# Attention, a dense FFN and a top-1 MoE in one kernel: routed weights in blocks of 128 rows, expert layers by halves, first expert's columns by tile, and products without readers in the last tile's waits

## The chip, the cores and the metric

The kernel runs on one core of one Trainium2 chip. The metric is the device time of one execution in microseconds, as the median of three runs. Engines are named as in the profile: PE (TensorE) does matrix products, PEld is the loading of their stationary operand, DVE, ACT and POOL are the vector, scalar and GpSimd engines, and SP issues most DMAs.

## The reference

Three layers follow each other on 1536 tokens of 512 numbers, all in fp32 accuracy.

```python
# 1 attention: B=2, H=8, S=768, D=64; a token sees 4 sinks and the last 128 positions
scores = where(is_sink | in_window, q @ k.T / sqrt(D), -1e9)
x = softmax(scores) @ v                       # -> [1536, 512]
# 2 dense FFN, w_in 512x2048, w_out 2048x512
h = x @ w_in
x = maximum(0.01 * h, h) @ w_out
# 3 routed, 8 experts, w1 512x1024, w2 1024x512
do_compute = x @ w_skip > 0
logits = x @ w_gate;  e = argmax(logits);  gate = softmax(logits)[e]
out = x + (do_compute ? gate * (maximum(x @ w1[e], 0) @ w2[e]) : 0)
```

## The kernel before

**Products.** Each operand is split into a rounded part (hi) and the rest (lo), and a product is three PE products: hi·hi, hi·lo and lo·hi. ACT (or POOL) writes the hi part and DVE (or POOL) the lo part (`split` for weights, lines 701 and 708; `split_psum`, lines 1094 and 1095).

**Order.** A planner (`Plan`) takes every operation with its engine, a modelled cost, the buffers it reads and writes and a due time `pr`, and makes one fixed order for each engine. The queues are in order: an instruction that waits holds back all behind it. Buffers are taken by tag and have few slots: 32 slots of split weights (`w`), 4 of raw weights (`wm`), 1 `vs`, 2 `wf`, and PSUM banks `acc` 2, `h` 2, `T` 2, `S` 1, `PV` 1.

**Dense layers.** Attention and the dense FFN go in six groups of 256 tokens (two tiles of 128 tokens), the FFN in chunks of its 2048 columns (`chunk`: lines 835 and 856). After a group its gating follows (`gating`): copy x out of PSUM (902 on ACT, 904 on DVE), transpose it (918), split it (921, 922), make nine logits a token (w_skip and eight gates) with twelve products a tile on a nine-column stationary operand (930), copy them (935), transpose them back (937), then on DVE the argmax chain (947 to 959) to a one-hot row (954), and on PE a count of earlier tokens with the same expert (977), from which DVE reads each token's place in its expert's list (983, `rank_all`). Finished rows are scattered to a list in HBM, 128 places an expert. The last group does this for its two tiles one after the other.

**First expert.** Expert 0's 128 rows would have to come back from that list. Instead the ten earlier tiles' rows come by an early load (`xs0`), and `first_x` adds the rows of the last two tiles on PE: four 128-column pieces of transposed x are the sum of a product with `xs0` (817) and of a product of each last tile with a 0/1 matrix `sel` (819), which DVE makes from the rank (987).

**Routed layers.** `plan_routed` runs the eight experts on 128 rows each: weights come in tiles of 512 KB (four for w1, four for w2; loads at 1037), are split (701, 708), x is loaded (1050; not for expert 0's products) and transposed (1059), the first layer is 24 products of 512 columns in two banks, hidden columns 0 to 511 and 512 to 1023 (1066), relu is done by ACT on the one and DVE on the other (1070, 1071), then eight transposes (1075), their split, 24 products of the second layer (1082), gate and residual (1085), and a scatter to the output.

Of the kernel before, what the change touches and what calls it, by code (L numbers as in the profile page):

```python
# [47 lines left out]
C_TR = 114.0  # L48
# [177 lines left out]
class Arm:  # L226
# [63 lines left out]
    def keep(self):  # L290

        k = lambda name, shape, dt=F32: self.pool.tile(shape, dt, tag=name, bufs=1, name=name)
        self.oh_all = k("oh_all", [128, self.NT // 128, self.E], BF16)
        self.rank_all = k("rank_all", [128, self.NT // 128])
        self.gate_all = k("gate_all", [128, self.NT // 128])
        self.nt = k("nt", [128, 2, self.E])
        self.tot = k("tot", [128, 2], I32)
        self.w9 = k("w9", [128, 2, 4, 9], F32R)
        self.ks = k("ks", [128, self.KD, 16])
# [393 lines left out]
    def split(self, src, dst, at, n, pr, hi="ACT", lo="DVE", view=lambda t: t):  # L693
# [12 lines left out]

        P.op(hi, {"ACT": c_act(n, False), "DVE": c_dve2(n), "POOL": c_pool1(n)}[hi], f_hi, r=[src], w=[hk], pr=pr)
        P.op(lo, {"DVE": c_dve(n), "POOL": c_pool2(n)}[lo], lambda: eng[lo].tensor_tensor(  # L708
            out=at(1), in0=view(src.tile), in1=at(0).bitcast(F32), op=ALU.subtract), r=[src, hk], w=[lk], pr=pr)
# [36 lines left out]
    def plan_dense(self):  # L746
# [50 lines left out]
        for step in self.rest:  # L797
            step()
# [11 lines left out]
    def first_x(self, x2):  # L810
# [4 lines left out]
        self.x0 = [P.buf(t, [128, 128]) for t in ("h", "h", "acc", "acc")]  # L815
        for k, x in enumerate(self.x0):
            P.op("PE", 220, lambda k=k, x=x: nc.tensor.matmul(out=x.tile, lhsT=xs0.tile[:, k:512:4], rhs=c["idt"], start=True, stop=False), r=[xs0], w=[x], pr=pr - 0.1)
        for k, x in enumerate(self.x0):
            P.op("PE", 440, lambda k=k, x=x: [nc.tensor.matmul(out=x.tile, lhsT=x2[i].tile[:, k:512:4], rhs=sel.tile[:, i, :], start=False, stop=i == 1) for i in range(2)],
                 r=[(x2[i], h) for i in range(2) for h in range(2)] + [(sel, 0), (sel, 1)], w=[x], pr=pr)  # L820
# [43 lines left out]
    def prepare(self, done):  # L864
# [9 lines left out]
        P.op("DVE", 90, lambda: nc.vector.tensor_copy(self.w9[:, 0], raw.tile), r=[raw], w=["w9"], pr=8)  # L874
        P.op("DVE", 100, lambda: nc.vector.tensor_tensor(out=self.w9[:, 1], in0=raw.tile, in1=self.w9[:, 0].bitcast(F32), op=ALU.subtract), r=[raw], w=["w9"], pr=8)
# [10 lines left out]
    def gating(self, g, acc, own):  # L886
# [9 lines left out]
        for i, t in zip(own, tiles):  # L896
            x = P.buf("x2", [128, 514])
            x2.append(x)
            for h in range(parts):
                q = slice(w * h, w * h + w)  # L900
                if (i if n > 1 else h) == 0:
                    P.op("ACT", c_act(w, True), lambda x=x, i=i, q=q: nc.scalar.activation(out=x.tile[:, q], in_=acc[i].tile[:, q], func=AF.Copy), r=[acc[i]], w=[(x, h)], pr=pr - 8)
                else:
                    P.op("DVE", c_dve(w), lambda x=x, i=i, q=q: V.tensor_copy(x.tile[:, q], acc[i].tile[:, q]), r=[acc[i]], w=[(x, h)], pr=pr - 8)
# [3 lines left out]
        lp = P.buf("T", [9, 128 * n])  # L908
        for m, x in enumerate(x2):
            tp = P.buf("T", [128, 512])  # L910
            xh = P.buf("wl", [128, 2, 512], F32R)
            for h in range(parts):
# [7 lines left out]
                P.op("PE", len(ks) * C_TR, tr, r=[(x, h)], w=[(tp, h)], pr=pr, hold=[xh])  # L920
# [3 lines left out]
            for h in range(parts):  # L924
                ks = range(4 // parts * h, 4 // parts * (h + 1))

                def lg(m=m, xh=xh, ks=ks):
                    for k in ks:
                        for j, (a, b) in enumerate(((0, 0), (1, 0), (0, 1))):
                            nc.tensor.matmul(out=lp.tile[:, 128 * m:128 * m + 128], lhsT=self.w9[:, a, k, :], rhs=xh.tile[:, b, 128 * k:128 * k + 128],  # L930
                                             start=k == 0 and j == 0, stop=k == 3 and j == 2)

                P.op("PE", 3 * len(ks) * 54, lg, r=[(xh, (0, h)), (xh, (1, h)), "w9"], w=[lp], pr=pr)
        ls = P.buf("wl", [9, 128 * n])
        P.op("ACT", c_act(128 * n, True), lambda: nc.scalar.activation(out=ls.tile, in_=lp.tile, func=AF.Copy), r=[lp], w=[ls], pr=pr)
        lt = P.buf("T", [128, n, 9])
        P.op("PE", 30 * n, lambda: [nc.tensor.transpose(lt.tile[:, m, :], ls.tile[:, 128 * m:128 * m + 128], c["idt"][0:9, 0:9]) for m in range(n)], r=[ls], w=[lt], pr=pr)
# [10 lines left out]
        d(70, lambda: V.tensor_scalar(out=v(act, 1), in0=lt.tile[:, :, 0:1], scalar1=0.0, scalar2=None, op0=ALU.is_gt), [lt], [(s, "act")])  # L948
        for m in range(n):
            d(80, lambda m=m: V.scalar_tensor_tensor(out=cand()[:, m, :], in0=lt.tile[:, m, 1:9], scalar=one(mx, m), in1=c["em"][:, 0, :], op0=ALU.is_equal, op1=ALU.mult),  # L950
              [lt, (s, "mx")], [(s, ("cand", m))])
        d(85, lambda: V.tensor_reduce(out=v(mi, 1), in_=cand(), op=ALU.min, axis=AX.X), [(s, ("cand", m)) for m in range(n)], [(s, "mi")])
# [18 lines left out]
        for m, x in enumerate(x2):  # L971
# [8 lines left out]
            for part in ([ts[:-1], ts[-1:]] if last else [ts]):  # L980
                P.op("PE", 30 * len(part), lambda part=part, count=count: count(part), r=[("oh", t) for t in part], w=[cp], pr=pr)
            rk = self.rank_all[:, tiles[m]:tiles[m] + 1]
            d(80, lambda m=m, rk=rk, cp=cp: V.tensor_tensor_reduce(out=cand()[:, m, :], in0=cp.tile, in1=oh(m), op0=ALU.mult, op1=ALU.add,
                                                                   scale=1.0, scalar=0.0, accum_out=rk), [cp, ("oh", tiles[m])], [(s, ("cand", m)), ("rank", tiles[m])])
            if last:
                i = own[0]
                d(133, lambda rk=rk, i=i: V.tensor_scalar(out=self.sel.tile[:, i, :], in0=self.sel.tile[:, 2, :], scalar1=rk,
                                                          scalar2=self.sel.tile[:, 3, i:i + 1], op0=ALU.is_equal, op1=ALU.mult),
                  [("rank", tiles[m]), (self.sel, 2), (self.sel, ("own", i))], [(self.sel, i)])
# [29 lines left out]
    def plan_routed(self):  # L1019
# [4 lines left out]
        def weights(e, m, pr):  # L1024
            src = io["moe2_w2"][e].rearrange("(p j) d -> p j d", j=8) if m else io["moe2_w1"][e].rearrange("(p k) f -> p k f", k=4)
            W[e, m] = []
            for n in range(4):
                sv = src[:, 2 * n:2 * n + 2, :].rearrange("p j d -> p (j d)") if m else src[:, n, :]
# [5 lines left out]
                for i in range(k):  # L1034
                    q = slice(1024 // k * i, 1024 // k * (i + 1))
                    raw = P.buf(tag, [128, 1024 // k])
                    P.op("SP", C_DMA, lambda raw=raw, sv=sv, q=q: nc.sync.dma_start(out=raw.tile, in_=sv[:, q]), w=[raw], pr=pr - 16, lat=512 * 1024 / 310.0 / k)
                    self.split(raw, [(x, i) for x in hl], lambda j, hl=hl, q=q: hl[j].tile[:, q], 1024 // k, pr + 0.3 * n, "ACT", "DVE" if n != 3 or e == self.E - 1 else "POOL")
# [4 lines left out]
        for e in range(self.E):  # L1043
            pr = N + 3.5 * e
            if e + 1 < self.E:
                weights(e + 1, 0, pr - 2.8)
            weights(e, 1, pr - 1.5)
# [6 lines left out]
            if e == 0:  # L1054
                for k, x in enumerate(self.x0):
                    self.split_psum(x, (xt, k), lambda i, xt=xt, k=k: xt.tile[:, i, k], 128, N - 9)
            else:
                tp = P.buf("acc", [128, 4, 128])
                P.op("PE", 4 * C_TR, lambda xs=xs, tp=tp: [nc.tensor.transpose(tp.tile[:, k, :], xs.tile[:, k:512:4], c["idt"]) for k in range(4)], r=[xs, ("g1", e - 1)], w=[tp], pr=pr - 3.48)
                self.split_psum(tp, xt, lambda i, xt=xt: xt.tile[:, i], 512, pr - 6)  # L1060
            hp = [P.buf(t, [128, 512]) for t in (("S", "PV"), ("h", "h"))[e % 2]]
            for k in range(4):
                def g1(k=k, xt=xt, hp=hp, w1=w1):
                    for a in range(2):
                        for n, (i, j) in enumerate(((0, 0), (0, 1), (1, 0))):
                            nc.tensor.matmul(out=hp[a].tile, lhsT=xt.tile[:, i, k, :], rhs=w1[k][j].tile[:, 512 * a:512 * a + 512],  # L1066
                                             start=k == 0 and n == 0, stop=k == 3 and n == 2)
                P.op("PE", 6 * c_mm(512), g1, r=([(xt, (k, 0)), (xt, (k, 1))] if e == 0 else [xt]) + [w1[k][0], w1[k][1]], w=hp + ([("g1", e)] if k == 2 else []), pr=pr + 0.01 * k)
# [4 lines left out]
            for b in range(2):  # L1073
                tp = P.buf("T", [128, 4, 128])
                P.op("PE", 4 * C_TR, lambda hs=hs, tp=tp, b=b: [nc.tensor.transpose(tp.tile[:, j, :], hs.tile[:, 4 * b + j:1024:8], c["idt"]) for j in range(4)], r=[hs], w=[tp], pr=pr + 0.065)
                self.split_psum(tp, (gt, b), lambda i, gt=gt, b=b: gt.tile[:, i, 4 * b:4 * b + 4, :], 512, pr - 3)
            yp = P.buf("acc", [128, 512])
            for n in range(4):
# [5 lines left out]
                P.op("PE", 6 * c_mm(512), g2, r=[(gt, (n // 2, 0)), (gt, (n // 2, 1)), w2[n][0], w2[n][1]], w=[yp], pr=pr + 3.55 + 0.01 * n)  # L1084
# [6 lines left out]
    def split_psum(self, src, dst, at, n, pr):  # L1091
        P, nc = self.p, self.nc
        hk, lk = self.halves(dst)
        P.op("ACT", c_act(n, True), lambda: nc.scalar.activation(out=at(0), in_=src.tile, func=AF.Copy), r=[src], w=[hk], pr=pr)
        P.op("DVE", c_dve(n), lambda: nc.vector.tensor_tensor(out=at(1), in0=src.tile, in1=at(0).bitcast(F32), op=ALU.subtract), r=[src, hk], w=[lk], pr=pr)
# [219 lines left out]
def constants(nc, cp, pool, c, n_sink, window, E):  # L1315
# [21 lines left out]

    G.iota(dif, pattern=[[-1, 128]], base=0, channel_multiplier=1, allow_small_or_imprecise_dtypes=True)
# [80 lines left out]
```

## Time and profile before

| | before |
|---|---|
| timed runs, us | 560.93, 560.33, 559.50; median 560.33 |
| profiled execution, us | 561.0 (its span in the trace 559.2) |
| PE busy | 521.8 us, 93% of the span |
| DVE, ACT, POOL busy | 74%, 62%, 30% |
| moved by DMA | 72.5 MB |
| up to 433 us | attention and the dense FFN, group by group |
| 433 to 457 us | from the last dense product to expert 0's second layer |
| 457 to 551 us | experts, then 8 us to the end of the span |

A time in the trace is counted from the span's start. A group of instructions on one line (x12) has one start and one busy time. In the chain of waits each piece is what the end of the program waited for at that time. In the timeline a number in brackets is idle time of the engine just before, with what ended it. The granted clock (PEclk, or the column of that name) is 1.00 at TensorE's upper level of 2.4 GHz and 0.50 at its lower of 1.2 GHz.

### The profile page before, as it was taken

What the parts mean: (1) busy time and instruction counts of PE and PEld (TensorE: products, weight loads), DVE (VectorE), ACT (ScalarE), POOL (GpSimd) and SP (SyncE); (2) the same over time, 40 slices, a digit from 0 to 9 for tenths busy, and PEclk for the clock granted to TensorE, in tenths of its full rate; (3) what the DMA queues carried; (4) which work ended last, traced back from release to release, by engine and by line L of the source; (5) the groups of instructions that cost most, each with busy time, mean ns of one, the idle gap of its engine ahead of it and who ended that gap; (6) DMA issues with size and microseconds to landing.
All of it is one profiled execution on the core that took longest, in us unless ns stands there. A gap on an engine that the chain in (4) does not pass through costs nothing.

```text
span 559.2 us, 10360 instructions
## 1 busy us (share of the span) xinstructions
PE 521.8 (93%) x3370; PEld 457.7 (82%) x3370; DVE 415.9 (74%) x1167; ACT 345.8 (62%) x899; POOL 166.9 (30%) x288
## 2 busy tenths in 40 slices
PE   3899999999998999989999999999999789999994
PEld 2778998888887888978888888988898668878883
DVE  3899999997667676777576876766856558998761
ACT  3998766655666656675556766465555367767650
POOL 4332022130264133333223333220221314354231
PEclk9999999999999999999999999999999899999998
DMA  7996344431111212232112320106565359879820
GB/s 179 308 349 234 130 154 139 136 104 38 50 39 30 68 30 45 50 83 49 29 24 51 85 49 16 24 1 221 164 213 184 128 193 319 301 236 353 277 79 19
DMA packets 80351, 72.46 MB, mean 130 GB/s; under 512 B 56563, under 2 KB 64755, under 8 KB 80288
## 3 DMA queue, kind: packets, MB, share of 16 engines
q1 hardware_dynamic: 78000, 70.54, 40.7%
q0 software_dynamic: 1600, 1.04, 0.6%
q8 instruction: 29, 0.48, 0.3%
q14 instruction: 34, 0.28, 0.2%
q10 hardware_dynamic: 688, 0.13, 0.1%
HBM read 65.40 MB, written 10.51 MB: 136 GB/s over the span
## 4 chain that ended last, share of the span: by engine, by line
PE 66%; DVE 14%; ACT 9%; issue 4%; DMA 3%; POOL 2%; POOLq 0%; SPq 0%; DVEq 0%; ACTq 0%
PE h L835 17%; PE acc L856 14%; PE acc L1082 7%; PE T L616 3%; PE PV L655 3%; PE h L1066 2%; DMA wm<-in_moe_w_dram 2%; PE S L1066 2%; PE PV L1066 2%; ACT P L588 2%; PE S L582 2%; DVE w L708 2%; PE T L930 1%; DVE C L671 1%; DVE P L585 1%
## 5 line engine op out<-in xcount | busy, mean ns | idle before, releaser
L835 PE MATMUL h<-x,w 128*128 128x256 f32 x1128 | 155.1, 286 | 0.1
L835 PEld LDWEIGHTS h<-x,w 128*128 128x128 f32 x1128 | 143.9, 190 | 4.3 <-DVE w L708 0.6
L856 PE MATMUL acc<-w,gh 128*128 128x512 f32 x308 | 100.2, 406 | 0.2 <-ACT gh L848 0.2
L588 ACT ACTIVATE P<-P,s 128x272 f32<-128x272 f32 (+1 forms) x96 | 50.2, 524 | 27.8 <-DVE s L585 26.4
L600 POOL TENSOR_SCALAR P<-P,s 128x272 f32<-128x272 f32 (+1 forms) x72 | 36.8, 523 | 93.8 <-DVE s L593 74.9
L856 PE MATMUL acc<-w,gl 128*128 128x512 f32 x156 | 61.5, 394 | 0.6 <-DVE gl L849 0.6
L856 PEld LDWEIGHTS acc<-w,gh 128*128 128x128 f32 x308 | 53.2, 189 | 7.9 <-ACT gh L848 0.6
L708 DVE TENSOR_TENSOR w<-wm,w 128x1024 fp32r<-128x1024 f32 x35 | 52.3, 1509 | 8.8 <-ACT w L701 8.0
L701 ACT ACTIVATE w<-wm 128x1024 fp32r<-128x1024 f32 x44 | 46.1, 1060 | 17.2 <-DMA wm<-in_moe_w_dram 6.8
L847 DVE TENSOR_TENSOR h<-h,t 128x256 f32<-128x256 f32 x94 | 40.2, 427 | 22.2 <-ACT t L846 21.7
L846 ACT ACTIVATE t<-h 128x256 f32<-128x256 f32 x94 | 35.7, 379 | 33.5 <-PE h L835 33.2
L848 ACT ACTIVATE gh<-h 128x256 fp32r<-128x256 f32 x92 | 34.9, 379 | 21.7 <-DVE h L847 20.9
L849 DVE TENSOR_TENSOR gl<-h,gh 128x256 fp32r<-128x256 f32 x92 | 38.6, 419 | 9.3 <-ACT gh L848 8.5
L701 ACT ACTIVATE w<-wf 128x512 fp32r<-128x512 f32 x52 | 31.8, 627 | 11.1 <-DVE wf L741 8.9
L585 DVE CUSTOM_DVE_ANT_0 P<-S,mk 128x272 f32<-128x272 f32 (+1 forms) x70 | 28.9, 413 | 11.3 <-PE S L582 7.9
L856 PEld LDWEIGHTS acc<-w,gl 128*128 128x128 f32 x156 | 29.3, 188 | 8.4 <-DVE gl L849 1.9
L708 POOL TENSOR_TENSOR w<-wm,w 128x1024 fp32r<-128x1024 f32 x9 | 22.3, 2477 | 44.5 <-PE h L835 15.2
L616 PE MATMUL T<-idt,P 128*128 128x128 f32 x152 | 27.2, 295 | 7.1 <-DVE kT L503 3.3
L616 PEld LDWEIGHTS T<-idt,P 128*128 128x128 f32 x152 | 22.3, 205 | 13.0 <-POOL P L600 4.3
L708 DVE TENSOR_TENSOR w<-wf,w 128x512 fp32r<-128x512 f32 x42 | 28.7, 694 | 0.7 <-ACT w L701 0.7
L671 DVE TENSOR_TENSOR C<-PV,C 64x256 f32<-64x256 f32 x48 | 20.3, 422 | 11.2 <-ACT C L670 8.1
L672 POOL TENSOR_TENSOR xr<-C 128x128 f32<-128x128 f32 x32 | 15.7, 490 | 43.0 <-DVE C L671 42.7
(267 smaller groups left out, 1117.0 us busy)
## 6 DMA issues: line engine op xcount, KB each, us to landing
wm<-in_moe_w_dram SPq DMA_DIRECT2D x44, 512.0 KB, 4.8
w<-in_moe_w_in_dram SPq DMA_DIRECT2D x14, 512.0 KB, 5.9
w<-in_moe_w_out_dram SPq DMA_DIRECT2D x14, 512.0 KB, 6.4
wf<-in_moe_w_dram SPq DMA_DIRECT2D x20, 256.0 KB, 5.0
vs<-in_moe_w_dram SPq DMA_DIRECT2D x10, 512.0 KB, 5.3
rq<-in_q_dram SPq DMA_DIRECT2D x56, 64.0 KB, 2.0
out_dram<-x SPq DMA_DIRECT2D x12, 256.0 KB, 2.9
rk<-in_k_dram SPq DMA_DIRECT2D x24, 96.0 KB, 2.1
```

The costliest lines, as they stand in the source:

```text
L588: P.op("ACT", 280 + 0.83 * ncol, lambda h=h: nc.scalar.activation(out=A.tile[:, 0:ncol, h], in_=A.tile[:, 0:ncol, h], func=AF.Exp, scale=- ...
L600: P.op("POOL", 245 + 0.83 * ncol, lambda h=h: nc.gpsimd.tensor_scalar(out=A.tile[:, 0:ncol, h], in0=A.tile[:, 0:ncol, h], scalar1=sm.tile[ ...
L616: nc.tensor.transpose(tt.tile[:, 2 * j + h, :], A.tile[:, o:o + 128, h], c["idt"])
L701: nc.scalar.activation(out=at(0), in_=view(src.tile), func=AF.Copy)
L708: P.op(lo, {"DVE": c_dve(n), "POOL": c_pool2(n)}[lo], lambda: eng[lo].tensor_tensor(out=at(1), in0=view(src.tile), in1=at(0).bitcast(F32), ...
L835: nc.tensor.matmul(out=h.tile, lhsT=wi.tile[:, a, 128 * k:128 * k + 128], rhs=xT.tile[:, b, k, :], start=k == 0 and n == 0, stop=k == self ...
L846: P.op("ACT", c_act(256, True), lambda: nc.scalar.activation(out=t.tile, in_=h.tile, func=AF.Copy, scale=0.01), r=[h], w=[t], pr=fast)
L847: P.op("DVE", c_dve(256), lambda: nc.vector.tensor_tensor(out=h.tile, in0=h.tile, in1=t.tile, op=ALU.max), r=[t], w=[h], pr=fast)
L848: P.op("ACT", c_act(256, True), lambda: nc.scalar.activation(out=gh.tile, in_=h.tile, func=AF.Copy), r=[h], w=[gh], pr=fast)
L849: P.op("DVE", c_dve(256), lambda: nc.vector.tensor_tensor(out=gl.tile, in0=h.tile, in1=gh.tile.bitcast(F32), op=ALU.subtract), r=[h, gh], ...
L856: nc.tensor.matmul(out=acc[i].tile, lhsT=a.tile[:, q], rhs=wo.tile[:, b, :], start=first and n == 0, stop=last and n == 2)
L1082: nc.tensor.matmul(out=yp.tile, lhsT=gt.tile[:, a, 2 * n + j, :], rhs=w2[n][b].tile[:, 512 * j:512 * j + 512], start=n == 0 and j == 0 and ...
```

## The change

1. **Logits.** The stationary operand holds hi and lo gate columns side by side (18 columns), so that a tile takes eight products, four on x's hi part and then four on its lo part, as operations of their own. One fp32 product with a constant `fold` (18x9, two identities) takes the place of the transpose back and adds the two halves. This holds for all six groups. In the last group the logits lie in a PV bank.
2. **Selection.** `sel` is computed from the count in PSUM, ahead of the rank. Expert 0's columns of x are taken in runs of 128, and the products of the first of the two last tiles with its `sel` go as operations of their own ahead of the second tile's; two of the four sums share one bank.
3. **Idle products.** `idle` adds seven bf16 products of 128x512 ones into a spare bank, which nothing reads, each behind a named operation and at the lowest priority.
4. **Weights.** w1 and w2 are read as blocks of 128 consecutive rows: a partition of a w1 tile still reads 4 KB in a piece, one of a w2 tile two pieces of 2 KB. The transposes read runs of 128 columns, no strided ones.
5. **Halves.** The first layer goes by output half: all twelve products of hidden columns 0 to 511, then those of 512 to 1023. A transpose needs its half alone. For expert 0 the first four transposes stand between the halves, and its second layer comes ahead of expert 1's first; its w2 is loaded ahead of expert 1's w1.
6. **Splits put off.** Two of expert 2's w1 tiles are split only after expert 0's x is, and one of them on DVE, not POOL.
7. A DVE copy of x waits for ACT's, and one DVE step of the argmax chain (`act`) moves back by one.

The rows below are the order of instructions on PE. First, from the end of the last dense products through the logits of the first of the two last tiles (x_1274 before; x_1287 is the other; T and PV hold transposed x and logits). Before:

```order
L817 MATMUL acc_6252<-idt,xs_5977 128x128
L918 MATMUL T_6256<-idt,x_1274_5913 128x128 x4
L856 MATMUL acc_5669<-w_1894,gh_6218 128x512 x2
L856 MATMUL acc_5669<-w_1894,gl_6227 128x512
L930 MATMUL T_6272<-wl_6257,w_75 9x128 x6
L817 MATMUL acc_6280<-idt,xs_5977 128x128
L930 MATMUL T_6272<-wl_6257,w_75 9x128 x6
L918 MATMUL T_6291<-idt,x_1287_5975 128x128 x4
```

After, at the same place:

```order
L929 MATMUL T_6207<-idt,x_1274_5875 128x128 x2
L866 MATMUL acc_5624<-w_1896,gh_6177 128x512 x2
L866 MATMUL acc_5624<-w_1896,gl_6189 128x512
L929 MATMUL T_6207<-idt,x_1274_5875 128x128 x2
L943 MATMUL PV_6220<-wl_6208,w_75 18x128 x2
L821 MATMUL acc_6223<-idt,xs_5939 128x128 x2
L943 MATMUL PV_6220<-wl_6208,w_75 18x128 x4
L830 LDWEIGHTS ones
L830 MATMUL acc_6234<-ones 128x512
```

The last three dense products stand ahead of the last two transposes and of the products with xs0; the logits are eight, and idle products (L830) stand among them.

Second, on PE, from the second tile's logits turned back to the first products with `sel` (hs is `sel`, oh_all the one-hot rows). Before, all eight products with `sel` follow the twelve of the overall count (L1007):

```order
L937 MATMUL T_6349<-idt,wl_6345 128x9
L977 LDWEIGHTS tri
L977 MATMUL PV_6331<-oh_all,tri 128x8
...
L819 MATMUL h_6189<-hs_5609,x_1274_5913 128x128
L819 MATMUL h_6189<-hs_5609,x_1287_5975 128x128
L819 MATMUL h_6234<-hs_5609,x_1274_5913 128x128
```

After:

```order
L951 MATMUL T_6295<-fold,wl_6274 128x9
L821 MATMUL h_6151<-hs_5546,x_1274_5875 128x128
L821 MATMUL h_6194<-hs_5546,x_1274_5875 128x128
L821 MATMUL acc_6223<-hs_5546,x_1274_5875 128x128 x2
L830 LDWEIGHTS ones
L830 MATMUL acc_6234<-ones 128x512
L992 LDWEIGHTS tri
L992 MATMUL PV_6280<-oh_all,tri 128x8
```

The four products of the first tile moved ahead of the second tile's count; the four of the second follow the overall count (now L1023). Of the dense groups, the order on each engine is the same up to the first group's gating and differs in places from there on.

The core of the diff:

```diff
+    def idle(self, n, done):
+        many = lambda: ones.rearrange("p (o n) -> p o n", o=1).to_broadcast([128, 4, 128])
+        for _ in range(n):
+            self.p.op("PE", 216, lambda: nc.tensor.matmul(out=x.tile..., lhsT=ones, rhs=many(), start=True, stop=True), w=[x], pr=self.KF * self.NG, after=[done])
...
# gating
-                        for j, (a, b) in enumerate(((0, 0), (1, 0), (0, 1))):
-                            nc.tensor.matmul(out=lp..., lhsT=self.w9[:, a, k, :], rhs=xh.tile[:, b, 128 * k:128 * k + 128], ...)
+            for b in range(2):
+                            nc.tensor.matmul(out=lp..., lhsT=self.w9[:, k, :, :].rearrange("p a e -> p (a e)"), rhs=xh.tile[:, b, 128 * k:128 * k + 128], ...)
+                    made = P.op("PE", len(ks) * 66, lg, r=[(xh, (b, h)), "w9"], w=[lp], pr=pr)
+                fill((1, 1)[b], made)
-        P.op("PE", 30 * n, ... nc.tensor.transpose(lt.tile[:, m, :], ls.tile[...], c["idt"][0:9, 0:9]) ...)
+        P.op("PE", 200 * n, ... nc.tensor.matmul(out=lt.tile[:, m, :], lhsT=ls.tile[...], rhs=c["fold"], start=True, stop=True) ...)
+        fill(2, P.ops[-1])
...
# plan_routed
-            src = io["moe2_w2"][e].rearrange("(p j) d -> p j d", j=8) if m else io["moe2_w1"][e].rearrange("(p k) f -> p k f", k=4)
+            src = io["moe2_w2"][e].rearrange("(j p) d -> p j d", j=8) if m else io["moe2_w1"][e].rearrange("(k p) f -> p k f", k=4)
...
-            for k in range(4):
+            for a in range(2):
+                for ks in ((0,), (1,), (2,), (3,)) if e == 0 and a == 0 else ((0, 1), (2, 3)):
...
-                P.op("PE", 4 * C_TR, ... hs.tile[:, 4 * b + j:1024:8] ..., r=[hs], w=[tp], pr=pr + 0.065)
+                P.op("PE", 4 * C_TR, ... hs.tile[:, 512 * b + 128 * j:512 * b + 128 * j + 128] ..., r=[(hs, b)], w=[tp], pr=pr + (0.065 if e else 0.01))
```

## Rows read from the trace of the kernel before

**Rows 1.** The page, parts 1 and 2: PE's busy time, its granted clock in 40 slices.

```profile
PE 521.8 (93%) x3370; PEld 457.7 (82%) x3370; DVE 415.9 (74%) x1167; ACT 345.8 (62%) x899; POOL 166.9 (30%) x288
...
PEclk9999999999999999999999999999999899999998
```

**Rows 2.** 2-us windows: busy PE, PEld, DVE, ACT, POOL, granted clock, DMA share, GB/s.

```profile
442.00:444.00 2.00, 1.11 (x16) 1.11 (x16) 1.93 (x18) 0.30 (x2) 1.00 (x1) 0.64 0.08 30
444.00:446.00 2.00, 2.00 (x11) 2.00 (x10) 1.29 (x9) 0.55 (x2) 0.00 (x0) 0.50 0.18 69
...
448.00:450.00 2.00, 2.00 (x7) 1.60 (x6) 0.00 (x0) 0.48 (x1) 0.00 (x0) 0.66 0.00 1
```

**Rows 3.** Timeline of PE, waits with their releasers.

```profile
440.13 0.88 PE L930 MATMUL T<-wl,w 128*9 128x128 f32 x12 [1.40 <-DVE sm L959]
...
442.88 0.17 PE L977 MATMUL PV<-oh_all,tri 128*128 128x8 bf16 x1 [1.22 <-DVE oh_all L954]
...
455.38 1.13 PE L1075 MATMUL T<-idt,hs 128*128 128x128 f32 x8 [1.52 <-ACT hs L1070]
```

**Rows 4.** Chain of waits, 433 to 462 us: start, duration, what.

```profile
434.24 0.73 PE acc L817 x2
434.98 0.44 PE T L918 x4
...
440.13 0.88 PE T L930 x12
...
443.37 2.10 PE h L819 x8
445.47 1.87 PE acc L819 x8
...
453.17 0.47 PE PV L1066 x2
...
456.75 1.91 PE acc L1082 x6
...
459.12 2.75 PE acc L1082 x12
```

**Rows 5.** Timeline of DVE at the last rank.

```profile
443.09 0.17 DVE L983 CUSTOM_DVE_ANT_0 sm<-PV,oh_all 128x8 f32<-128x8 f32 x1
...
443.30 0.34 DVE L987 TENSOR_SCALAR hs<-hs,rank_all 128x128 f32<-128x128 f32 x1
```

**Rows 6.** Chain of waits of the whole run, a dense group's logits.

```profile
392.17 1.44 PE T L930 x24
```

**Rows 7.** Timelines of SP's queue and of ACT: weights around expert 0.

```profile
451.86 0.34 SPq L1037 DMA_DIRECT2D vs<-in_moe_w_dram  x1
...
449.52 1.06 ACT L701 ACTIVATE w<-vs 128x1024 fp32r<-128x1024 f32 x1 [1.85 <-PE PV L1066]
```

**Rows 8.** Windows of the experts and of one earlier stretch, columns as in rows 2.

```profile
460.00:480.00 20.00, 19.83 (x100) 16.43 (x98) 18.08 (x19) 15.71 (x22) 8.57 (x5) 1.00 0.88 299
480.00:500.00 20.00, 18.79 (x89) 15.43 (x89) 19.53 (x20) 14.01 (x19) 8.85 (x6) 1.00 0.81 271
500.00:520.00 20.00, 20.00 (x101) 16.85 (x100) 17.06 (x18) 13.03 (x18) 11.89 (x6) 1.00 0.96 341
520.00:540.00 20.00, 20.00 (x95) 16.65 (x94) 15.43 (x20) 13.38 (x19) 5.55 (x4) 1.00 0.62 201
96.00:100.00 4.00, 4.00 (x26) 3.55 (x25) 4.00 (x11) 2.12 (x6) 1.52 (x3) 1.00 1.04 303
```

**Rows 9.** Chain of waits among the experts: a relu behind splits on DVE.

```profile
478.43 2.52 DVE w L708
...
492.15 0.61 DVE hs L1071
```

**Rows 10.** The page, part 6: loads of 512 KB, us from issue to landing.

```profile
w<-in_moe_w_in_dram SPq DMA_DIRECT2D x14, 512.0 KB, 5.9
w<-in_moe_w_out_dram SPq DMA_DIRECT2D x14, 512.0 KB, 6.4
```

More of the change, by code (lines that the diff above doesn't have):

```diff
@@ L691, in halves, with split @@
         return [(dst[0], (dst[1], i)) if isinstance(dst, tuple) else (dst, i) for i in range(2)]
-    def split(self, src, dst, at, n, pr, hi="ACT", lo="DVE", view=lambda t: t):
+    def split(self, src, dst, at, n, pr, hi="ACT", lo="DVE", view=lambda t: t, after=()):
         P, nc = self.p, self.nc
@@ L705, in f_hi @@
                 nc.gpsimd.tensor_scalar(out=at(0), in0=view(src.tile), scalar1=1.0, scalar2=1.0, op0=ALU.mult, op1=ALU.mult)
-        P.op(hi, {"ACT": c_act(n, False), "DVE": c_dve2(n), "POOL": c_pool1(n)}[hi], f_hi, r=[src], w=[hk], pr=pr)
+        P.op(hi, {"ACT": c_act(n, False), "DVE": c_dve2(n), "POOL": c_pool1(n)}[hi], f_hi, r=[src], w=[hk], pr=pr, after=after)
         P.op(lo, {"DVE": c_dve(n), "POOL": c_pool2(n)}[lo], lambda: eng[lo].tensor_tensor(
@@ L797, in plan_dense @@
         for step in self.rest:
-            step()
+            done = step()
+        self.spare = self.p.buf("acc", [128, 512])
+        self.idle(2, done)
         self.first_x(x2 + self.gating(g, acc, [1]))
@@ L814, in first_x @@
         xs0, sel = self.xs0, self.sel
[L815 to L820, printed above, removed]
+        two = P.buf("acc", [128, 2, 128])
+        self.x0 = [(x, None, lambda x=x: x.tile) for x in (P.buf("h", [128, 128]) for _ in range(2))] + [(two, j, lambda j=j: two.tile[:, j, :]) for j in range(2)]
+        for m, (x, cols) in enumerate([(xs0, lambda: c["idt"])] + [(x2[i], lambda i=i: sel.tile[:, i, :]) for i in range(2)]):
+            for k, x0 in enumerate(self.x0):
+                P.op("PE", 260, lambda k=k, x=x, x0=x0, m=m, cols=cols: nc.tensor.matmul(out=x0[2](), lhsT=x.tile[:, 128 * k:128 * k + 128], rhs=cols(), start=m == 0 and k < 3, stop=m == 2 and k != 2),
+                     r=[(x, h) for h in range(2)] + [(sel, m - 1)] if m else [xs0], w=[x0[0:2]], pr=pr + (0.2, 0.1, 0)[m])
+        self.idle(0, P.ops[-1])
+    def idle(self, n, done):
+        nc, ones, x = self.nc, self.c["ones"], self.spare
+        many = lambda: ones.rearrange("p (o n) -> p o n", o=1).to_broadcast([128, 4, 128])
+        for _ in range(n):
+            self.p.op("PE", 216, lambda: nc.tensor.matmul(out=x.tile.rearrange("p (o n) -> p o n", o=4), lhsT=ones, rhs=many(), start=True, stop=True), w=[x], pr=self.KF * self.NG, after=[done])
     def chunk(self, g, f, acc, xT):
@@ L907, in gating @@
                  r=[(x, h) for h in range(parts)], w=[("out", t)], pr=pr - 20, lat=1000)
-        lp = P.buf("T", [9, 128 * n])
+        fill = (lambda k, done: self.idle(k, done)) if last and own == [1] else (lambda k, done: None)
+        lp = P.buf("PV" if last else "T", [18, 128 * n])
         for m, x in enumerate(x2):
@@ L1036, in weights @@
                     raw = P.buf(tag, [128, 1024 // k])
-                    P.op("SP", C_DMA, lambda raw=raw, sv=sv, q=q: nc.sync.dma_start(out=raw.tile, in_=sv[:, q]), w=[raw], pr=pr - 16, lat=512 * 1024 / 310.0 / k)
-                    self.split(raw, [(x, i) for x in hl], lambda j, hl=hl, q=q: hl[j].tile[:, q], 1024 // k, pr + 0.3 * n, "ACT", "DVE" if n != 3 or e == self.E - 1 else "POOL")
+                    P.op("SP", C_DMA, lambda raw=raw, sv=sv, i=i, k=k: nc.sync.dma_start(
+                        out=raw.tile.rearrange("p (j d) -> p j d", d=512), in_=sv[:, i:i + 1, :] if k == 2 else sv), w=[raw], pr=pr - 16, lat=512 * 1024 / 310.0 / k)
+                    self.split(raw, [(x, i) for x in hl], lambda j, hl=hl, q=q: hl[j].tile[:, q], 1024 // k, pr + 0.3 * n, "ACT", "DVE" if n != 3 or e == self.E - 1 or (e, m) == (2, 0) else "POOL",
+                               after=[first] if (e, m) == (2, 0) and n > 1 else ())
                 W[e, m].append(hl)
```

84 lines of the change are left out of this document (45 added, 39 removed).

## The prediction

> **What bounds the kernel now.** I read the page first: PE is busy 93% of the span and its granted clock is at the upper level in all slices but one [rows 1]. So time is to be had where PE waits or runs at the lower clock, or from PE work that falls away. The windows show where that is. Around 442 us PE is busy 1.11 of 2 us and its clock falls to a mean of 0.64; from 444 to 446 it is at 0.50 (1.2 GHz) with PE full, and it is back in the window from 448 to 450 [rows 2]. That stretch is the passage from the last dense products to the experts: the two last tiles are gated, sel is made, expert 0's columns are formed. PE's timeline shows its three waits there: 1.40 us for DVE, 1.22 us for the second one-hot row, and 1.52 us for expert 0's relu [rows 3]. The chain of waits runs through the same pieces [rows 4]. Behind it, from 460 us on, PE is full in three of four windows and lacks 1.2 us in the one from 480 to 500, where DVE is busy 19.53 of 20 us [rows 8].
>
> **The passage, term A.** I follow the chain and take differences.
>
> 1. The last accumulator's products stand behind two products with xs0 (0.73 us) and four transposes (0.44 us, so 0.11 each) [rows 4]. After the change they stand behind two transposes alone: 0.73 + 0.22, −1.0 us. The moved products go into the wait for DVE, which now comes before them.
> 2. Logits of the second tile: twelve products take 0.88 us, 0.073 each, after the lo part is there [rows 4]. After, only four of eight wait for the lo part (0.29 us): −0.6, of which I keep −0.5, since an idle product may end just after the lo part.
> 3. sel no longer waits for the rank (443.09 to 443.30 [rows 5]): −0.2 us.
> 4. The eight products with sel take 2.10 + 1.87 = 3.97 us at the lower clock [rows 4]. Four of them move into the 1.22 us wait of rows 3. An fp32 product of 128 columns takes 0.73 / 2 = 0.365 us at the upper clock [rows 4], so the four that remain take 1.46 us: −2.5 us. The four that move take 1.46 us of a wait of 1.22, and an idle product stands behind them (a 512-column product is 2.75 / 12 = 0.229 us [rows 4]): +0.4 us to the second tile's count.
> 5. `fold` has no row. It takes as little as the transpose that it replaces (0) and at most an fp32 product of 128 columns, 0.365 us; with nine columns I take +0.2.
> 6. Expert 0's 24 products run from 447.34 (445.47 + 1.87) to 453.64, 6.30 us, the first ones at the lower clock [rows 4]. At 0.229 us they are 5.5: −0.8 us.
> 7. From 453.64 to the first product of the second layer at 456.75 there are 3.11 us [rows 4]: relu, eight transposes, a split. After, the first four transposes stand between the products, where relu of that half has six products (1.4 us) to hide in; they cost their 0.45 us there. At the end there remain relu (0.61 [rows 9]), about 0.3 us of issue and four transposes, 1.35 us; the split of the last half hides behind twelve products. Together 1.8 us: −1.3.
>
> The sum is −1.0 −0.5 −0.2 −2.5 +0.4 +0.2 −0.8 −1.3 = −4.7, and items 4 and 6 hold only if the clock stays up. Item 1 has a second effect: the first wait in rows 3, 1.40 us for DVE, is itself made of the first tile's chain, which loses its own logits (another 0.6 us) and the products with xs0 that stood between its two halves (0.73 us in the row at 434.24, and as much again later). I take −1.0 of these 1.3. **A = −5.7 us.** The seven idle products are 7 × 0.229 = 1.6 us of PE, of which I have counted 0.23. The others stand in the waits of rows 3, 2.6 us in all for DVE, and cost nothing; if that cover goes, they cost up to 1.4 us. With the size of fold I give A ±0.9.
>
> **The five earlier groups, term B.** There PE is the bound, so work that falls away counts whole. Sixteen logits products stand for 24, which take 1.44 us, 0.06 each [rows 6]: 8 × 0.06 = 0.48 us a group. Two folds cost 0 to 0.73 us a group more than the transposes. That is −2.4 to +1.2 us for five. Here other products stand around a fold and its load can hide behind them, so I take 0.13 us a fold, less than in item 5: 5 × (0.26 − 0.48), **B = −1.1**.
>
> **The experts, term C.** Here the change gives little and may take. Before, the first split that waited for a free weight slot ran at 449.52, 2.2 us after the first product of expert 0, and the loads began again at 451.86; for some us before that nothing was moved [rows 7, 2]. By halves, a w1 slot is free only once the second half has used it: after 18 products, 4.1 us. With A's first five items that is at about 447.8, so loads begin some 1.8 us earlier by the clock. But two tiles of expert 2's w1, which sit unsplit in raw buffers, leave 1 MB more to load, 3.0 us at the 341 GB/s by a share of 0.96 of rows 8. So weights come 1.2 us later, and PE wants them 5.7 us earlier: 6.9 us less lead. The unused DMA share from 460 to 500 is 20 × (0.12 + 0.19) = 6.2 us [rows 8]. So the lead is just about used up where PE already lacks 1.2 us. DVE gets one more split of 1.2 us (half of the 2.52 us pair in rows 9) in place of POOL, but in the time before 450, when it has room (1.29 of 2 us [rows 2]). Half-wise transposes, contiguous reads and expert 0's earlier second layer speak for a little gain, at best those 1.2 us and some tenths. From −1.5 to +4.0, I take **C = +1.0**, near the lower end, since the arithmetic ends close to zero.
>
> A rule speaks against the w2 layout. The trace has two loads of 512 KB with different pieces: w_in, in pieces of 1 KB, lands after 5.9 us, and w_out, in pieces of 4 KB, after 6.4 [rows 10]: no loss from smaller pieces. The Trainium skill (Perfetto Trace Analysis, DMA Optimizations) says that small DMAs, under 2 KB, have a significant overhead and that going from 2 KB to 4 KB or 8 KB "can dramatically improve throughput". By the row w2 costs nothing; by the rule the time would go to the second rival below.
>
> **The dense order, term D.** New costs in the planner change the order from the first gating on. Nothing of it is aimed; 0 ± 1.5.
>
> **Sum.** −5.7 −1.1 +1.0 = −5.8 us on the profiled execution's 561.0 gives 555.2. The median of the runs, 560.33, lies 0.67 below that execution, so the forecast is 554.5.
>
> **Rivals.** *The clock falls all the same.* Before, it fell after waits of 1.40 and 1.22 us [rows 3]; the idle products fill part of such waits, perhaps not enough. Then the products with sel take 0.50 us each, as in rows 4, not 0.365: 8 × 0.135 = 1.1 us; expert 0's first products lose 0.8; two idle products double, 0.5. That is +2.4: 556.9. Against it stands that the waits are also shorter by items 1 to 3.
>
> *w2 in pieces of 2 KB makes the DMA the bound.* The one stretch with pieces of about 2 KB (a list of 2056-byte rows filled from 96 us on, writes) moved 303 GB/s at a share of 1.04, 291 at a full one; 500 to 520 with 4 KB pieces moved 341 at 0.96, 355 [rows 8]. Half of some 22 MB at the lower rate costs 11 MB × (1/291 − 1/355) = 6.8 us. With the lead of term C used up, 3 to 5 us of it reach PE: 558.5, with rows 10 against it.
>
> *Slower: relu behind splits on DVE.* In rows 9 relu on DVE stands behind 2.52 us of splits, and DVE's queue is in order; PE's eight transposes wait for it. If weights come 6.9 us later against PE, more of their splits fall into the time when relu is due. Price: 1.2 us for one split, 2.5 for two, in each of six experts. A and B come to −6.8, and this takes the place of C; so it is slower than before from 1.15 us an expert on, and by over 0.3% from 1.45. With two splits in four of six experts it is 10.1 − 6.8 = +3.3: 563.6. Against it: DVE lacks only 0.5 to 2 us of full from 460 to 500, but has 3 to 4.6 us to spare in each 20 from 500 on [rows 8], so it should fade after three experts.
>
> **How the numbers follow.** About 0.3%, 1.7 us, is what a measurement of this kernel tells from no change, so faster means under 558.65. Chances: the forecast 0.70, the clock falls 0.15, 2 KB pieces 0.09, relu behind splits 0.06. The forecast's own spread from A ±0.9, B ±1.8, C ±2.5 and D ±1.5, taken as independent, is ±3.5: 551.0 to 558.0, which holds the first rival too. Above lie the other two (0.15) and a little of the forecast's edges. Faster: 0.70 + 0.15 and a third of the second rival, less 0.02 for the upper edge, 0.86; within 0.3%: two thirds of the second rival and that edge, 0.08; slower: 0.06.
>
> **What would show it.** Clock: 1.00 in every window from 436 to 456, or a dip as before. Passage: the first second-layer product of expert 0 at about 450 us (456.75 − 5.7 − 1.1). Item 7: under 2 us between the last of expert 0's first-layer products and that one. B: 16 logits products a group, and the start of the last group's gating 1 us earlier. C: from that product to the end of the span, 102.4 us before (456.75 to 559.2), about a microsecond more now; PE windows under 19 of 20 there with DMA at full share speak for the second rival, with DVE full and relu as releaser for the third. The prediction is wrong if the dense groups move by more than 2 us, or if what the passage gains is waited for again among the experts.

## The result

The changed kernel takes 550.9 us (median of 549.70, 551.51, 550.30 and 552.93) against 559.99 for the kernel before; the ratio is 0.9838 (0.981 to 0.9865). So it is 9.1 us faster, where 5.8 were forecast, and 0.1 us below the range of 551.0 to 558.0. The profiled execution of before is one of its longest (561.0), that of after its shortest (549.7). The two traces differ by 11.2 us, 2.1 more than the medians, and the stages below are to be read with that.

The page of the changed kernel, parts 1 and 2, answers to [rows 1]:

```profile
span 548.0 us, 10288 instructions
PE 517.1 (94%) x3341; PEld 452.8 (83%) x3341; DVE 411.6 (75%) x1168; ACT 344.3 (63%) x899; POOL 164.5 (30%) x288
...
PEclk9999999999999999999999999999999999999998
```

PE is busy 4.7 us less, and only the last slice, where PE's work has ended, is below 9 tenths of the clock (in [rows 1] it is that slice and one more, the passage). Windows of the changed kernel, columns as in rows 2 and 8:

```profile
436.00:438.00 2.00, 1.94 (x23) 1.66 (x22) 1.95 (x17) 0.41 (x4) 0.00 (x0) 1.00 0.00 0
438.00:440.00 2.00, 1.98 (x25) 1.57 (x24) 1.75 (x15) 0.52 (x4) 1.00 (x1) 1.00 0.16 53
...
460.00:480.00 20.00, 20.00 (x100) 16.52 (x99) 16.30 (x20) 15.31 (x22) 7.25 (x5) 1.00 0.94 336
480.00:500.00 20.00, 20.00 (x99) 16.61 (x98) 16.52 (x20) 12.80 (x17) 9.54 (x6) 1.00 0.85 286
```

Where [rows 2] had a clock of 0.64 and 0.50 it is 1.00 now, and where [rows 8] had PE at 18.79 and DVE at 19.53 of 20 us, they have 20.00 and 16.52. The chain of waits, to be held against [rows 4]:

```profile
432.23 0.49 PE acc L821 x4
...
437.12 0.64 PE h L821 x4
437.76 0.45 PE acc L821 x4
...
439.03 0.71 PE h L821 x4
439.74 0.45 PE acc L821 x4
440.19 2.90 PE S L1086 x12
443.09 1.36 PE PV L1086 x6
444.45 0.44 PE T L1096 x4
444.89 1.41 PE PV L1086 x6
446.30 0.02 issue
446.32 0.70 DVE hs L1092
447.02 0.04 issue
447.07 0.66 PE T L1096 x4
447.72 2.77 PE acc L1103 x12
```

From four starts in PE's timeline (the first dense product, the first product with xs0, the first of expert 0's first layer, the first of its second layer) and the two ends, the stages of both traces in us:

| stage | before | after | moved | forecast |
|---|---|---|---|---|
| to the first dense product | 24.80 | 25.12 | +0.3 | 0 |
| to the first product with xs0 (dense, terms B and D) | 403.14 | 399.56 | −3.6 | −1.1 |
| to expert 0's first layer (term A, items 1 to 5 and item 1's second effect) | 19.06 | 15.35 | −3.7 | −4.6 |
| to its second layer (items 6, 7) | 9.75 | 7.45 | −2.3 | −2.1 |
| to the end of the last second-layer product (C) | 94.66 | 92.33 | −2.3 | +1.0 |
| to the end of the span | 7.79 | 8.19 | +0.4 | 0 |

The forecasts are those of the single steps. Term A's come to −6.7, not to the −5.7 that the prediction states, because its eight items add up to −5.7 and not to −4.7, before the second effect of −1.0; A measured −6.0. The rest of the gain is in the dense groups, which were forecast too small, and among the experts, where a loss was forecast.

### The profile page after: what moved, and what is told of

Its sections match the earlier page's. It is cut to its first block, busy times and chain, and to the rows that moved or that the text cites. A ratio compares the mean times of both kernels' runs of the same rounds, so it can differ in the third digit from the quotient of the medians.

```text
span 548.0 us, 10288 instructions
## 1 busy us (share of the span) xinstructions
PE 517.1 (94%) x3341; PEld 452.8 (83%) x3341; DVE 411.6 (75%) x1168; ACT 344.3 (63%) x899; POOL 164.5 (30%) x288
## 2 busy tenths in 40 slices
DMA packets 83806, 72.44 MB, mean 132 GB/s; under 512 B 56563, under 2 KB 64755, under 8 KB 83744
## 4 chain that ended last, share of the span: by engine, by line
PE 74%; DVE 11%; ACT 7%; issue 3%; POOL 2%; DMA 2%; POOLq 0%; SPq 0%; ACTq 0%; DVEq 0%
PE h L845 19%; PE acc L866 15%; PE acc L1103 8%; PE h L1086 4%; PE PV L655 4%; PE T L616 3%; PE S L1086 2%; PE PV L1086 2%; PE S L582 2%; DVE C L671 2%; ACT P L588 2%; PE S L866 2%; PE PV L866 2%; DVE kT L503 1%; PE T L1096 1%
## 5 line engine op out<-in xcount | busy, mean ns | idle before, releaser
L708 DVE TENSOR_TENSOR w<-wm,w 128x1024 fp32r<-128x1024 f32 x36 | 49.3, 1376 | 3.8 <-ACT w L701 3.2
L708 POOL TENSOR_TENSOR w<-wm,w 128x1024 fp32r<-128x1024 f32 x8 | 19.7, 2461 | 41.8 <-ACT w L701 21.1
L622 ACT ACTIVATE AT<-T 128x256 fp32r<-128x256 f32 x60 | 20.1, 382 | 12.1 <-PE T L616 11.3
```

## The experiments

**Without the idle products.**

```diff
-        self.idle(2, done)
-        fill = (lambda k, done: self.idle(k, done)) if last and own == [1] else (lambda k, done: None)
+        fill = lambda k, done: None
```

> The changed kernel without its seven idle products; the order of all else on the engines is that of the changed kernel. Theory 1 (the idle products keep the clock up): the granted clock falls to 0.50 between 435 and 447 us as in the kernel before, the eight products with sel go from 0.27 to 0.50 us each and expert 0's first ones lose 0.8, so 2 to 3 us more than the changed kernel: 553 to 554. Rival (the waits are now so short that the clock stays up without them): 550.4 to 551.2, the same as the changed kernel or 0.5 less.

Measured: 551.9 us (550.61 to 552.16), ratio 0.984 to before. Windows of this kernel:

```profile
434.00:436.00 2.00, 1.47 (x11) 0.78 (x11) 1.24 (x8) 0.80 (x4) 0.00 (x0) 1.00 0.07 26
436.00:438.00 2.00, 1.73 (x21) 1.67 (x21) 1.95 (x17) 0.41 (x4) 0.00 (x0) 0.95 0.00 0
438.00:440.00 2.00, 1.84 (x21) 1.63 (x20) 1.79 (x15) 0.35 (x3) 0.99 (x1) 0.50 0.16 53
440.00:442.00 2.00, 2.00 (x10) 1.80 (x10) 1.19 (x8) 1.33 (x5) 0.00 (x0) 0.70 0.14 54
```

The clock does fall, to 0.50, so the idle products are what keeps it up; the mean clock of all four executions is 0.990 to 0.992, of the changed kernel's 0.994 to 0.997. By the windows it is at the lower level for 3.4 us in all, against 6.8 in the kernel before (442 to 450 us). Why the stretch is shorter isn't shown: the kernel before without splits on POOL, further down, has the passage of before and 3.4 us too (0.88, 0.50 and 0.76 in its windows from 442 to 448 us). From the first product with xs0 to expert 0's second layer the trace is 0.6 us longer than the changed kernel's; the medians, 1.0 apart, lie within the scatter of the times. Theory 1 holds in kind; its price of 2 to 3 us, my first rival's 2.4, was far too high for the stretch that came.

**Old logits in the new order.** Groups 0 to 4 have twelve products and the transpose back again, in the changed kernel's order.

```diff
+                            for a in range(2 - b):
+                                nc.tensor.matmul(out=lp.tile[0:9, ...], lhsT=self.w9[:, k, a, :], rhs=xh.tile[:, b, ...], ...)
```

> The changed kernel in its own order, but with twelve nine-column logits products a tile and the transpose back in the five earlier groups. Theory (the dense groups gained 3.3 us by less PE work): 40 products at 0.06 us come back and folds turn into transposes, 2.0 to 2.4 us more: about 553. Rival (it was the other order of the dense groups): within 0.5 us of the changed kernel, and the products with xs0 still start 3 us earlier than before.

Measured: 551.23 us (550.73 to 551.97). Its dense stage takes 400.66 us (25.15 to 425.81 in PE's timeline), 1.1 more than the changed kernel's 399.56 and 2.5 less than before. So in the trace the work is worth 1.1 us, as term B said, and neither theory nor rival is whole: 2.5 us of the dense gain are in the order. The times, 0.3 us apart, would fit the rival and are too scattered to tell.

**w2 in pieces of 4 KB.**

```diff
-            src = io["moe2_w2"][e].rearrange("(j p) d -> p j d", j=8) if m else ...
+            src = io["moe2_w2"][e].rearrange("(p j) d -> p j d", j=8) if m else ...
```

> The changed kernel with w2 loaded as before, in pieces of 4 KB a partition instead of two of 2 KB; the rows that then lie in a tile are not those of its hidden columns, all else is the changed kernel's. Theory (the 2 KB pieces cost nothing, the DMA has slack among the experts): 550.4 to 551.4, the same as the changed kernel. Rival (2 KB pieces cost DMA time that reaches PE): 1 us or more below the changed kernel, with a lower DMA share from 448 to 520.

Measured: 550.46 us (550.26 to 552.68). Among the experts the trace has 93.43 us, of which PE waited 1.0 for the load of expert 1's x; without that it is the changed kernel's 92.3. The page counts 83806 DMA packets for the changed kernel and 80350 for this one: 3456 apart, one for each of 128 partitions in 27 of the 32 w2 tiles. The other five come in halves, in pieces of 2 KB in every kernel here. From 448 to 520 us the DMA moved 301 GB/s at a share of 0.88 in the changed kernel and 297 at 0.88 in this one, so pieces of 2 KB cost nothing, neither in rate nor on PE. [rows 10], from which the prediction took this, is a poor witness: in the changed kernel's page the same two loads land after 7.4 us (pieces of 1 KB) and 6.5. The Trainium skill (Perfetto Trace Analysis, DMA Optimizations) says that larger transfers, 4 KB instead of 2 KB, can improve throughput dramatically, and puts this first where the DMA is the bound. Here PE is the bound, and the rate did not rise with the larger pieces.

**Experts by k, not by halves.**

```diff
+            for k in range(4) if e else ():
+                    for a in range(2):
```

> The changed kernel, but experts 1 to 7 do their first layer as before, both output halves for each block of x's columns; expert 0 and the dense groups keep order and work. Theory (the gain of 2.6 us among the experts comes from the halves, which let relu of the first half run under the products of the second): PE waits for relu again in several experts, 1 to 3 us more: 552 to 554. Rival (the gain comes from splits on DVE that are no longer stretched beside POOL's at 487 us, and from expert 0): within 0.5 us of the changed kernel.

Measured: 550.99 us (549.45 to 552.93), and 92.31 us among the experts. The theory fails: in experts 1 to 7 the halves bring nothing. The rival's number holds; its cause, the splits, is not tested by this run.

**The kernel before, logits as two operations for the planner** (in groups 0 to 4, eight products on the hi part, four on the lo part).

```diff
-                P.op("PE", 3 * len(ks) * 54, lg, r=[(xh, (0, h)), (xh, (1, h)), "w9"], w=[lp], pr=pr)
+                    for s in range(2):
+                        P.op("PE", len(ks) * 66, lg, r=[(xh, (s, h)), "w9"], w=[lp], pr=pr)
```

> The kernel before, with its twelve logits products a tile in the five earlier groups handed to the planner as two operations (eight on the hi part, four on the lo part) instead of one; the work is the same. The planner then orders the dense groups much as in the changed kernel. Theory (2.5 of the 3.6 us that the dense groups gained are this other order): the products with xs0 start 2 to 3 us earlier after the first dense product than in the kernel before (403.1 us there), and the time is 557.5 to 558.5. Rival (the gain is the eight products instead of twelve and the fold): 403 us there, 560 to 561.

Measured: 556.45 us (555.89 to 557.18), ratio 0.9937 (0.9917 to 0.9957), 3.4 us less than before (559.84) with not one product fewer. The dense stage takes 399.33 us; all later stages are those of before (19.05, 9.60, 94.65). The theory holds in kind; the gain is more than it named, and the time below its 557.5 to 558.5.

**The changed kernel, logits as one operation.**

```diff
+                    if b == 0: hold = lg
+                    else: made = P.op("PE", 2 * len(ks) * 66, lambda ...: [hold(), lg()], r=[(xh, (0, h)), (xh, (1, h)), "w9"], w=[lp], pr=pr)
```

> The changed kernel with its eight logits products a tile in the five earlier groups as one operation; the work is that of the changed kernel, the order of the dense groups close to that of the kernel before. Theory (the order is worth 2.5 us): the products with xs0 start 2 to 3 us later after the first dense product than the changed kernel's 399.6, and the time is 552.5 to 554. Rival (less work): within 0.7 us of the changed kernel, 550 to 551.6.

Measured: 553.51 us (551.13 to 554.02), 2.6 above the changed kernel. The profiled execution starts its first dense product 1.7 us late (26.80 us; see the last section), so the 2.6 are not the order's alone. The dense stage, counted from that product, takes 401.72 us (to 428.52), 2.2 more than the changed kernel's. Timeline of PE, waits of 0.9 us and more from 242 to 260 us, in this kernel:

```profile
248.29 0.71 PE L616 MATMUL T<-idt,P 128*128 128x128 f32 x4 [1.76 <-POOL xr L672]
258.02 0.72 PE L616 MATMUL T<-idt,P 128*128 128x128 f32 x4 [0.92 <-POOL P L600]
```

The kernel before has the same two:

```profile
246.24 0.71 PE L616 MATMUL T<-idt,P 128*128 128x128 f32 x4 [1.76 <-POOL xr L672]
255.98 0.71 PE L616 MATMUL T<-idt,P 128*128 128x128 f32 x4 [0.90 <-POOL P L600]
```

The changed kernel has one in their place, for the lo part of the logits:

```profile
245.49 0.66 PE L943 MATMUL T<-wl,w 128*18 128x128 f32 x8 [1.34 <-DVE wl L933]
```

As two operations the logits may be placed apart, and all attention work behind them moves. Two waits for POOL in attention go with it and a shorter one comes, 1.3 us of the 2.2. The whole dense stage in one window each (stretch, its length, busy PE, and the rest as in rows 2): the kernel before, before with two operations, the changed kernel with one operation, with old logits, and as it is:

```profile
24.80:427.94 403.14, 389.80 (x2698) 349.46 (x2697) 308.00 (x960) 257.71 (x740) 113.14 (x225) 1.00 0.32 97
24.77:424.10 399.33, 388.87 (x2699) 349.90 (x2697) 306.75 (x960) 258.29 (x740) 112.47 (x225) 1.00 0.33 98
26.80:428.52 401.72, 388.39 (x2668) 348.65 (x2667) 306.69 (x960) 258.36 (x740) 113.04 (x225) 1.00 0.33 97
25.15:425.81 400.66, 389.25 (x2699) 349.69 (x2698) 307.34 (x960) 258.26 (x740) 112.66 (x225) 1.00 0.33 98
25.12:424.68 399.56, 388.31 (x2668) 349.01 (x2667) 307.07 (x960) 257.87 (x740) 112.12 (x225) 1.00 0.33 99
```

Length less busy time is PE's idle time: 13.3, 10.5, 13.3, 11.4 and 11.3 us. So the order shows as idle time (13.3 in the two with the old order, 10.5 to 11.4 in the three with the new), and the work as busy time, 0.9 us between the last two.

**The kernel before, no split of routed weights on POOL.**

```diff
-  ..., "ACT", "DVE" if n != 3 or e == self.E - 1 else "POOL")
+  ..., "ACT", "DVE")
```

> The kernel before with all splits of routed weights on DVE, none on POOL. In the kernel before a 1024-column split on DVE takes 1.21 us alone and 2.9 to 4.1 us where POOL works beside it (473, 478 and 487 us), and the relu behind the last of these lets PE wait 1.2 us. Theory (POOL beside DVE stretches its splits and is what the experts lost): no split on DVE over 1.5 us among the experts, no wait of PE at 490, the stretch from the first second-layer product to the last 93.3 instead of 94.7 us. Rival (DVE has more to do and becomes the bound): PE waits for DVE more than 1.4 us there, 94.7 us or more.

Measured: 559.73 us (558.85 to 560.59), ratio 0.999 (0.9978 to 1.0003). PE's waits for relu on DVE among the experts of the kernel before (total, times, longest in us); this kernel has none:

```profile
PE T L1075 <- DVE hs L1071: 1.4, 2, 1.2
```

Timeline of DVE in the kernel before; splits of 1024 columns, which take 1.21 us elsewhere:

```profile
473.11 2.91 DVE L708 TENSOR_TENSOR w<-vs,w 128x1024 fp32r<-128x1024 f32 x1 [0.29 <-ACT w L701]
...
478.35 3.35 DVE L708 TENSOR_TENSOR w<-wm,w 128x1024 fp32r<-128x1024 f32 x1
...
487.50 4.06 DVE L708 TENSOR_TENSOR w<-wm,w 128x1024 fp32r<-128x1024 f32 x1 [0.47 <-ACT w L701]
```

And of POOL's splits at those times:

```profile
472.52 2.41 POOL L708 TENSOR_TENSOR w<-wm,w 128x1024 fp32r<-128x1024 f32 x1
...
478.22 2.40 POOL L708 TENSOR_TENSOR w<-wm,w 128x1024 fp32r<-128x1024 f32 x1 [3.29 <-ACT w L701]
...
487.92 2.54 POOL L708 TENSOR_TENSOR w<-wf,w 128x512 fp32r<-128x512 f32 x2
```

Without POOL's splits, DVE's at that place:

```profile
484.50 1.22 DVE L708 TENSOR_TENSOR w<-wm,w 128x1024 fp32r<-128x1024 f32 x1
488.06 2.35 DVE L708 TENSOR_TENSOR w<-wm,w 128x1024 fp32r<-128x1024 f32 x2
490.39 1.22 DVE L708 TENSOR_TENSOR w<-wm,w 128x1024 fp32r<-128x1024 f32 x1
```

In the trace the theory holds: no split is stretched, PE doesn't wait for relu at 490, and the experts take 93.15 us against 94.66. The time, though, is that of before; by the ratio's interval the gain is at most 1.2 us. The one profiled execution is at the lower end of its times (558.98). It is one of two with a mean granted clock of 0.993; the other eight have 0.985 to 0.991, so they ran longer at the lower level, which is at least a part of what they lose. How much isn't shown.

**Expert 1's x transposed later.**

```diff
-  r=[xs, ("g1", e - 1)], w=[tp], pr=pr - 3.48)
+  r=[xs, ("g1", e - 1)] + (["late"] if e == 1 else []), w=[tp], pr=pr - 3.48)
```

> The changed kernel with expert 1's x transposed after 18 of expert 0's 24 second-layer products instead of after 12. In two of four profiles of variants of the changed kernel PE waited 0.9 to 1.0 us there for the load of x (xs from the list), in two not at all. Theory (this wait is what scatters the changed kernel's times): no such wait, median 550 to 550.5 and a narrower spread. Rival (the scatter lies in the start of the kernel, before the first dense product): as the changed kernel, 550.4 to 551.4, with the same spread.

Measured: 552.37 us (551.57 to 553.18). No wait for the load any more; PE's waits after it, in all:

```profile
PE T L1096 <- DVE hs L1092: 1.7, 2, 0.9
PE h L1086 <- DVE wl L1117: 1.0, 1, 1.0
```

The first row is relu (0.8 us in the changed kernel, for expert 0 alone), the second the split of the x that comes late. The experts take 94.60 us. The move trades a wait of 1 us in some executions for some 2 us in the one traced; the narrower spread came with a higher median, so it says nothing on the cause of the scatter.

**fold made on DVE, and the changed kernel again.**

```diff
-    G.tensor_tensor(out=fold, in0=idt[0:18, 0:9], in1=idt[0:18, 9:18], op=ALU.add)
+    nc.vector.tensor_tensor(out=fold, in0=idt[0:18, 0:9], in1=idt[0:18, 9:18], op=ALU.add)
```

> The changed kernel with the constant for fold made on DVE instead of POOL, all else in the same order. In the changed kernel this operation stands on POOL ahead of the constants that PE's first transposes wait for: the first dense product starts at 25.0 to 25.3 us in five profiles of its variants and at 26.7 and 26.8 in two, where the products from 14 to 19 us take 1.7 times as long; it starts at 24.8 in all profiles of the kernel before and its variants. Theory (the operation on POOL shifts the start and brings the slow start about): first dense product at 24.8, times 549.0 to 550.5 without the upper group over 551. Rival (the slow start comes by chance, with either): times from 549.5 to 553 as the changed kernel has them, median 550.5 to 551.

> The changed kernel itself once more, in the same rounds as the one with fold on DVE: median 550.5 to 551.3, single times in two groups, 549.5 to 550.5 and 551.5 to 553.

Measured: 550.4 us (549.46 to 550.82) with fold on DVE, 551.06 (549.71 to 551.88) for the changed kernel in the same rounds; ratios to before 0.9837 (0.9818 to 0.9856) and 0.9853 (0.9835 to 0.9871). The intervals overlap: the lower median speaks for the theory and doesn't prove it, and the upper group is all but missing in the changed kernel too (one time of five above 551.5). The first dense product came at 24.97 us, not 24.8. This is the version to keep, though it isn't shown to beat the changed kernel.

## Why the prediction was right and wrong

**Right in mechanism, near in number by luck: the passage, A = −5.7.** The two stages gained 3.7 and 2.3 us, 6.0 in all. But the eight items add up to −5.7, not −4.7, and with the second effect of −1.0 the prediction's own terms give −6.7. The slip in adding stands in for 0.9 us that items 1 to 5 and that effect promised and did not give; which of them fell short isn't separated. Item 4: the four remaining products with sel take 0.71 + 0.45 = 1.16 us (1.46 forecast, from half of the 0.73 us in [rows 4]; that x2 is one product, which the trace records as two matmuls, as it records the eight products with sel as sixteen). Item 6: the 24 products 5.67 us without the transposes between them (5.5). Item 7: 0.44 us between the halves and 1.42 from 446.30 to 447.72, 1.86 (1.8). The clock is 1.00 throughout.

**Right: the work of the dense groups, B = −1.1.** Old logits in the new order cost 1.1 us; new ones in nearly the old order gain 1.4 (401.72 against 403.14). In the fifth group's rows sixteen products take 1.12 us for 1.60, as forecast, and two folds 0.61 for the 0.28 of two transposes.

**Wrong: the dense order, D = 0 ± 1.5.** This is the step that failed. "Nothing of it is aimed" was true and no bound: splitting one operation in two reorders PE in the dense groups, and a new order is worth 2.5 us by the old logits in the new order, 2.2 by one operation, and 3.8 in the dense stage (3.4 in time) by two operations in the kernel before. The prediction bounded it without a row; the idle time that stood to be lost or won, 13.3 us of PE in the dense stage, with waits of 1.76 and 0.90 us for POOL among it, was in the trace. Its own sign of being wrong came: the dense groups moved by 3.6 us, more than 2.

**Wrong in sign: the experts, C = +1.0.** The lead of the weights was not used up. ACT's longest wait for a load among the experts is longer than before, but its waits for loads there come to 2.9 us in all, against 5.7. The longest, in the timeline of ACT in the changed kernel (2.1 us before):

```profile
455.33 1.06 ACT L701 ACTIVATE w<-vs 128x1024 fp32r<-128x1024 f32 x1 [2.65 <-DMA vs<-in_moe_w_dram]
```

No such wait reaches PE. What fell away are PE's waits for relu, 1.4 us with the one of 1.2 behind a stretched split, and about 0.5 us in expert 0's first six second-layer products (1.91 us in [rows 4] against half of 2.77 now); the other 0.4 isn't placed. I had read the 2.52 us in [rows 9] as a pair of splits; it is part of one, of 3.35 us at 478.35, beside POOL. So I took DVE for nearly full by its work, when part of its 19.53 us was stretch. The changed kernel still has stretched splits (2.71 us at 450.58, 2.31 at 480.97), but none where PE waits for relu. That the better alignment is what saved the waits fits the run without POOL's splits; in the times no run shows it. The contrary case, the third rival, thereby lost its ground. The first rival did not come; the idle products prevent it, and without them it cost 0.6 us in the trace rather than 2.4. The second rival is refuted by w2 in pieces of 4 KB.

Taken together, D and C account for the miss: with −2.5 and −2.3 in place of 0 and +1.0, −6.0 for A, and +0.7 at the start and the end of the span, the sum is the −11.2 of the two traces. Added rightly, A would have made the forecast 553.5, with a range of 550.0 to 557.0 that holds 550.9, by an A that is 0.7 too large and with D and C just as wrong. The repeat of the changed kernel, 551.06, lies just inside the range as it was stated.

## What to carry to other kernels

Where a planner orders the work, a change in how an operation is cut is a change of all that follows: its gain is to be bounded by the waits in the stages that it reorders, not by the work that it removes, and it can be tried by itself, with the work unchanged. Before an engine is called full, its instructions of one kind are to be compared with each other: a split that takes three times as long as its like is waiting for something. A few idle products in short waits can hold the clock up; what they are worth is to be read from traces with and without them (here 0.6 us), not from how slow the products were before. And a slip in a sum of many small terms moves the whole range: here by 1.0 us, more than the miss.

## What the runs showed of the hardware

An elementwise operation on DVE of 1.21 us took 2.9 to 4.1 where POOL worked on two tensors at the same time, and none was stretched once POOL had no splits. That looks like waiting, not sharing: the three above end 1.09, 1.08 and 1.10 us after POOL's split does (476.02, 481.70 and 491.56 us against 474.93, 480.62 and 490.46), even the third, which by the record began 0.42 us ahead of POOL's. Three in the changed kernel (from 450.58, 480.97 and 489.72 us) end 1.08 to 1.10 us after POOL's too. In two of the first seven traces of the changed kernel and its variants (w2 in 4 KB pieces, one operation) the kernel's start takes 1.6 us longer, with the granted clock recorded as 1.00 and the same products slower; PE's timeline with w2 in 4 KB pieces, and then of the changed kernel:

```profile
14.90 1.22 PE L655 MATMUL PV<-AT,w 128*128 128x128 f32 x4
15.91 1.06 PE L616 MATMUL acc<-idt,P 128*128 128x128 f32 x4
```

```profile
14.72 0.71 PE L655 MATMUL PV<-AT,w 128*128 128x128 f32 x4
15.27 0.64 PE L616 MATMUL acc<-idt,P 128*128 128x128 f32 x4
```

None of the three traces of the kernel before and its variants shows it. With the 0.9 to 1.0 us that PE waits for the load of expert 1's x in some executions, it is as large as the scatter of the changed kernel's times. Its cause stays open. A lower clock that the column doesn't record would fit and isn't shown: 1.7 is near the factor of the products with sel at the lower clock (0.50 us against 0.28), and in the fast start too the first products are slow (the four from 9.89 us take 1.54 us, the four of the same line and size from 15.75 take 0.61), with the column at 1.00.
